# Reading a weight matrix in short contiguous runs in one stage of a fused decode kernel

## The chip, the cores and the metric

The kernel runs on one core of one Trainium2 chip. The metric is device time in microseconds (us) of one execution. A "fast run" is an execution whose time lies close to the fastest of the same kernel; only fast runs are compared.

## The reference, cut to what matters

```python
x = A_x; xn = layernorm(x)
return x + A(xn, k_cache, v_cache, wq, wo) + B(xn, w1, w2, w3, w4)

# A: one decode step of attention; batch 4, 32 query heads on 16 KV heads, window 2048, head size 128
#    softmax(q k^T / sqrt(128)) v, then @ wo          (k and v: 33.5 MB each in the window)
# B: x1 = x + shift(gelu(layernorm(x) @ w1)) @ w2
h2 = gelu(layernorm(x1) @ w3) @ w4                    # w3: 576 x 4608, w4: 4608 x 576
return x1 + h2
```

All data are bf16. With four rows of activations almost every byte that is loaded is used once: 88.5 MB come from HBM.

## The kernel before

One queue of loads (issued by SyncE) fills a ring of four positions with K chunks 1 to 16, then V chunks 1 to 16, 2 MB each. TensorE (PE) transposes each K chunk, ScalarE and VectorE copy it out of PSUM, and PE computes the scores. A ring position is loaded again when its last chunk has been transposed:

```python
for c in range(NC):     # NC = 16, NPOS = 4
    add_dma(kv_pairs(A_k_cache, c), ("k", c % NPOS), [t_done(c - NPOS)] if c >= NPOS else [], c)
for c in range(NC):
    add_dma(kv_pairs(A_v_cache, c), ("v", c % NPOS), [f"PV{c - NPOS}" if c >= NPOS else t_done(c + NC - NPOS)], KS + c)
```

So the fifth K chunk can be asked for only when PE has finished with the first. The MLP stage B stands on PE ahead of the K loop. Its second layer (h2) multiplies by w3, which lies in SBUF as rows of 4608 columns. w4 is loaded later in five pieces, whose partitions hold 18, 9, 6, 2 and 1 consecutive rows of w4. To match that order the kernel gathers columns of w3: for one row of w4 per partition it reads every 18th (9th, 6th, ...) column.

```python
W4_ROWS = (18, 9, 6, 2, 1)
H2ps = [ps[:, 4 + k, 0:384] for k in range(3)]
...
def pe_h2(r):                                   # r: one of 5 blocks of up to 128 rows of w3
    def f(e):
        for g, k, off, cnt, base_, rc, rr, first in sorted(segs, key=lambda x: (x[1], x[2], x[0])):
            w, x_ = ...                         # [cut]
            ins = e.matmul(H2ps[k][32 * g:32 * g + 32, 128 * off:128 * (off + cnt)].rearrange("p (c x) -> p c x", c=cnt), lhsT=x_,
                           rhs=w.rearrange("p (x s) -> p s x", s=rc)[:, rr:rr + cnt, :], start=(r == 0 and first), stop=(r == 3),
                           tile_position=(0, 32 * g), skip_group_check=True)
        return ins
    return f
for n, r in enumerate((0, 1, 4, 2, 3)):         # blocks 2 and 3 need the second half of w3
    add("pe", pe_h2(r), waits=[ev_w3[r // 2]] + ...)
# then: three GELUs (ScalarE), nine 128x128 transposes (PE), and the K loop
```

`tile_position=(0, 32 * g)` runs the four matmuls of a group side by side, so four streams are read at once: in the trace the first four start within 0.01 us of one another, and the records overlap (65 matmuls of 0.76 us each on average fill 11.1 us).

## Time and profile before

215.10 us median of six runs (214.99 to 215.34). The table is read from the page and the timeline of the kernel before.

| what | value |
|---|---|
| bytes loaded, mean rate over the span | 88.65 MB, 415 GB/s |
| PE, VectorE, ScalarE busy | 68%, 35%, 28% of the span |
| h2 matmuls (65) | 4.48 + 6.63 = 11.1 us |
| nine transposes of h2 | 0.68 us |
| K loop starts; fifth K chunk is issued | 38.8 us; 45.2 us |

From the page, the busy times and the 40 slices of the span (a digit is the busy share in tenths):

```profile
PE 144.9 (68%) x2639; PEld 110.3 (52%) x2643; DVE 75.3 (35%) x147; ACT 60.3 (28%) x76; POOL 10.9 (5%) x38
...
PE   0048698899999999999997077233444433336985
...
PEclk9999999699999999999999755555555555555899
DMA  7999999999999999999999999999999999999993
GB/s 282 406 383 449 435 415 436 426 420 425 433 429 420 429 433 433 422 429 429 423 429 433 423 429 423 421 436 426 426 423 436 426 423 426 433 429 429 427 413 129
```

The DMA engines are full in every slice but the first and the last. No engine comes near that over the whole span, but PE is as full in the 13 slices from 43 to 112 us, which lie in the K loop.

The chain of waits that ended last, its end (start us, length us, what):

```profile
178.12 32.27 DMA w<-in_B_w_dram
...
210.43 1.35 PE ps L433 x18
211.78 0.43 DVE out_sb L554
```

The last thing that the kernel waits for is a piece of w4. The timeline where the change acts (start us, length us, engine, line, operation, shapes, count, and in brackets the engine's idle time just before, with what ended it):

```profile
24.68 4.48 PE L517 MATMUL ps<-w,x1nT 128*32 128x384 bf16 x26 [0.38 <-DMA w<-in_B_w_dram]
...
30.06 6.63 PE L517 MATMUL ps<-w,x1nT 128*32 128x384 bf16 x39
...
36.74 1.25 ACT L526 ACTIVATE PT<-ps 128x384 bf16<-128x384 f32 x3 [10.17 <-remote]
...
38.05 0.68 PE L532 MATMUL ps<-ident_bf,PT 128*128 128x128 bf16 x9 [1.36 <-ACT PT L526]
...
38.82 3.45 PE L335 MATMUL ps<-perm_bf,ring 128*128 128x128 bf16 x32
...
45.18 9.90 SPq L175 DMA_DIRECT2D ring<-in_A_k_cache_dram  x3
```

L517 are the h2 matmuls, L526 the GELUs, L532 the transposes of h2, L335 the first transposes of K. The last line is the queue: at 45.18 it issues the fifth K chunk.

### The profile page before, as it was taken

The page shows a single profiled execution, that of the slowest core. Times are in us where ns is not written, and L with a number is a line of the kernel's source. Part 1 is how long each engine was busy: PE and PEld are TensorE (multiplying, and loading weights), DVE is VectorE, ACT ScalarE, POOL GpSimd, SP SyncE. Part 2 cuts the span into 40 slices and gives each one's busy share as a digit, 9 for nine tenths or more (in the row PEclk, how much of TensorE's full clock was granted, in tenths as well). Part 3 has the DMA queues.
Part 4 walks back from the last instruction along what each step waited for, and adds up shares of the span by engine and source line. Part 5 has one row for each costly group of instructions (what it writes and reads, how often), then busy time and mean ns, then how long its engine had stood idle before and what let it go on. Part 6 is the DMA issues. An engine that isn't in the chain of part 4 may idle for free. (4 is left out here: it accounts for less than half of the span.)

```text
span 213.6 us, 5856 instructions
## 1 busy us (share of the span) xinstructions
PE 144.9 (68%) x2639; PEld 110.3 (52%) x2643; DVE 75.3 (35%) x147; ACT 60.3 (28%) x76; POOL 10.9 (5%) x38
## 2 busy tenths in 40 slices
PE   0048698899999999999997077233444433336985
PEld 0023332778888877888885047233434433334542
DVE  0243600366677677667764741100010001001000
ACT  2001401355666665566666540000000000000000
POOL 8301000001000000100000000000000000000000
PEclk9999999699999999999999755555555555555899
DMA  7999999999999999999999999999999999999993
GB/s 282 406 383 449 435 415 436 426 420 425 433 429 420 429 433 433 422 429 429 423 429 433 423 429 423 421 436 426 426 423 436 426 423 426 433 429 429 427 413 129
DMA packets 6690, 88.65 MB, mean 415 GB/s; under 512 B 780, under 2 KB 1048, under 8 KB 1560
## 3 DMA queue, kind: packets, MB, share of 16 engines
q1 hardware_dynamic: 6664, 88.50, 97.8%
q8 instruction: 8, 0.13, 0.2%
q14 instruction: 2, 0.02, 0.0%
q10 hardware_dynamic: 16, 0.01, 0.0%
HBM read 88.49 MB, written 0.00 MB: 414 GB/s over the span
## 5 line engine op out<-in xcount | busy, mean ns | idle before, releaser
L335 PEld LDWEIGHTS ps<-perm_bf,ring 128*128 128x128 bf16 x1024 | 59.0, 99 | 7.2 <-issue 7.0
L335 PE MATMUL ps<-perm_bf,ring 128*128 128x128 bf16 x1024 | 62.0, 222 | 0.1
L342 DVE COPY kt<-ps 128x1024 bf16<-128x1024 bf16 x80 | 52.4, 688 | 24.5 <-PE ps L335 23.3
L416 PE MATMUL ps<-PTpad,ring 128*128 128x8 bf16 x1024 | 29.7, 168 | 40.6 <-PEq L578 36.8
L341 ACT ACTIVATE kt<-ps 128x1024 bf16<-128x1024 bf16 x48 | 47.6, 1023 | 29.9 <-PE ps L335 29.9
L416 PEld LDWEIGHTS ps<-PTpad,ring 128*128 128x128 bf16 x1024 | 28.7, 104 | 41.7 <-issue 41.6
L555 ACT ACTIVATE out_sb<-ps 4x288 bf16<-4x288 f32 x1 | 0.4, 401 | 86.6 <-PE ps L433 86.6
L349 PE MATMUL ps<-kt,Qs 128*32 128x512 bf16 x272 | 17.8, 382 | 1.4 <-PEq L578 1.4
L405 DVE TENSOR_TENSOR PTpad<-PT,mU_bf 128x512 bf16<-128x512 bf16 x16 | 6.4, 422 | 29.0 <-PE ps L416 29.0
L428 DVE TENSOR_TENSOR OTn<-ps,rinvB 128x32 bf16<-128x32 f32 x4 | 0.8, 192 | 34.2 <-PE ps L416 34.2
L517 PE MATMUL ps<-w,x1nT 128*32 128x384 bf16 (+1 forms) x65 | 11.1, 760 | 0.4 <-DMA w<-in_B_w_dram 0.4
L276 PE MATMUL ps<-ident_bf,xn_bf 4*128 4x4 bf16 x8 | 0.6, 170 | 13.8 <-DVE ragsrc L270 13.8
L349 PEld LDWEIGHTS ps<-kt,Qs 128*32 128x32 bf16 x272 | 5.8, 95 | 6.8 <-issue 1.5
L370 POOL COPY Qs<-Qpad 128x128 bf16<-128x128 bf16 x16 | 4.6, 296 | 88.2 <-PE ps L349 74.7
L276 PEld LDWEIGHTS ps<-ident_bf,xn_bf 4*128 4x128 bf16 x8 | 0.4, 112 | 13.9 <-issue 11.5
L517 PEld LDWEIGHTS ps<-w,x1nT 128*32 128x32 bf16 x65 | 3.6, 109 | 5.4 <-issue 4.7
L433 PE MATMUL ps<-w,h2T_sb 128*4 128x288 bf16 x72 | 4.9, 286 | 1.3 <-DMA w<-in_B_w_dram 1.3
L554 DVE CAST out_sb<-ps 4x288 bf16<-4x288 f32 x1 | 0.4, 446 | 14.5 <-PE ps L433 14.5
L433 PE MATMUL ps<-w,ORT 128*4 128x288 bf16 x64 | 4.9, 321 | 0.4 <-DVE ORT L455 0.4
L387 PE MATMUL ps<-kt,permT_bf 128*128 128x512 bf16 x3 | 1.8, 609 | 4.9 <-DVE kt L386 4.8
L433 PEld LDWEIGHTS ps<-w,h2T_sb 128*4 128x4 bf16 x72 | 2.9, 84 | 3.7 <-DMA w<-in_B_w_dram 2.7
L538 DVE COPY h2T_sb<-ps 128x16 bf16<-128x16 bf16 x1 | 0.2, 166 | 13.0 <-PE ps L532 13.0
(99 smaller groups left out, 63.5 us busy)
## 6 DMA issues: line engine op xcount, KB each, us to landing
ring<-in_A_k_cache_dram SPq DMA_DIRECT2D x16, 2048.0 KB, 12.3
ring<-in_A_v_cache_dram SPq DMA_DIRECT2D x16, 2048.0 KB, 17.1
w<-in_B_w_dram SPq DMA_DIRECT2D x2, 2304.0 KB, 22.6
w<-in_A_wo_dram SPq DMA_DIRECT2D x2, 2304.0 KB, 20.6
kt<-in_A_wq_dram SPq DMA_DIRECT2D x1, 4096.0 KB, 12.5
w<-in_B_w_dram SPq DMA_DIRECT2D x1, 2592.0 KB, 28.0
w<-in_B_w_dram SPq DMA_DIRECT2D x3, 576.0 KB, 13.9
w<-in_B_w_dram SPq DMA_DIRECT2D x1, 1296.0 KB, 30.6
```

Source lines behind the costliest of these rows:

```text
L276: e.transpose(XTps[idx][:, r, :], v[:, r, :], ident_bf[0:B, 0:B])
L335: ins = e.transpose(tb[n % 4][:, t, :], slot_t(c)[:, 8 * k + t, :], perm_bf[:])
L341: return "act", lambda e: e.activation(out=ktbuf[:, n % 16], in_=tb[n % 4], func=ACTF.Copy)
L342: return "dve", lambda e: e.tensor_copy(out=ktbuf[:, n % 16], in_=tb[n % 4])
L349: ins = e.matmul(Sps[32 * u:32 * u + 32, q, :].rearrange("p (t i) -> p t i", t=16), lhsT=Qs[:, c % NPOS, 32 * u:32 * u + 32], rhs=ktgrp[:, ...
L370: P(lambda e, c=c, cc=cc: e.tensor_copy(out=Qs[:, c % NPOS, :], in_=Qpad_t[:, 128 * cc:128 * cc + 128]), waits=["qT", "qs_zero"] + ([f"SC{ ...
L387: add("pe", lambda e, q=q: e.matmul(ps[:, 4 + q % 3, :], lhsT=permT_bf[:], rhs=PTx[:, q, :], start=True, stop=True), waits=[f"PTx{q}", "pe ...
L405: return lambda e: e.tensor_tensor(out=PTpad[:, c % 2], in0=PTv[:, :, cc, :].unsqueeze(2).to_broadcast([128, NT, NU, 2]), in1=mU_bf[:].uns ...
L416: ins = e.matmul(o_, lhsT=slot_t(c)[:, t, :], rhs=PTpad[:, c % 2, t].rearrange("p u e -> p (u e)"), start=(t == 0), stop=(t == NT - 1))
L428: add("dve", lambda e, hv=hv: e.tensor_tensor(out=hv(OTn), in0=OTps.rearrange("p (b h) -> p b h", b=B), in1=hv(rinvB), op=ALU.mult), waits ...
L433: return e.matmul(ACC[h], lhsT=lhsT, rhs=rhs, start=start, stop=stop, tile_position=(0, 32 * h), skip_group_check=True)
L517: ins = e.matmul(H2ps[k][32 * g:32 * g + 32, 128 * off:128 * (off + cnt)].rearrange("p (c x) -> p c x", c=cnt), lhsT=x_, rhs=w.rearrange(" ...
```

## The change

It exchanges the order of the two inner loops of the read. A matmul takes a third of the positions x (43, 43 or 42) and for each of them up to nine neighbouring columns, so w3 is read in runs of 9 (or 6, 2, 1). PSUM and the GELU's output are then ordered by position first, and each transpose takes every ninth column. There are 90 h2 matmuls instead of 65. No load changes.

```diff
+        XS = (0, 43, 86, 128)
+        H2ps = [ps[:, 4 + k, 0:9 * (XS[k + 1] - XS[k])] for k in range(3)]
...      # segs: runs of up to 9 columns of one row group of w4, no longer cut in threes
+                for k in range(3):
+                    for g, off, cnt, base_, rc, rr in sorted(segs, key=lambda x: (x[1], x[0])):
-                    ins = e.matmul(H2ps[k][32 * g:32 * g + 32, 128 * off:128 * (off + cnt)].rearrange("p (c x) -> p c x", c=cnt), lhsT=x_,
-                                   rhs=w.rearrange("p (x s) -> p s x", s=rc)[:, rr:rr + cnt, :], start=(r == 0 and first), stop=(r == 3),
+                        ins = e.matmul(H2ps[k][32 * g:32 * g + 32, :].rearrange("p (x c) -> p x c", c=9)[:, :, off:off + cnt], lhsT=x_,
+                                       rhs=w[:, base_:base_ + 128 * rc].rearrange("p (x s) -> p x s", s=rc)[:, XS[k]:XS[k + 1], rr:rr + cnt],
+                                       start=(r == 0 and off == 0), stop=(r == 3), ...
-            ... out=h2g[:, 384 * k:384 * (k + 1)], in_=H2ps[k], func=ACTF.Gelu_apprx_tanh
+            ... out=h2g[:, 9 * XS[k]:9 * XS[k + 1]], in_=H2ps[k], func=ACTF.Gelu_apprx_tanh
-                ins = e.transpose(..., h2g[:, 128 * j:128 * j + 128], ident_bf[:])
+                ins = e.transpose(..., h2g[:, j:1152:9], ident_bf[:])
```

More of the change, by code (lines that the diff above doesn't have):

```diff
@@ L140, in bass_parallel_sum__sliding_block_cached__mixer_s_mlp__decode_kernel @@
         QTps = ps[:, 6, :].bitcast(BF16)
-        H2ps = [ps[:, 4 + k, 0:384] for k in range(3)]
+        XS = (0, 43, 86, 128)
+        H2ps = [ps[:, 4 + k, 0:9 * (XS[k + 1] - XS[k])] for k in range(3)]
         H2Ta = ps[:, 7, :].bitcast(BF16)
@@ L499, in bass_parallel_sum__sliding_block_cached__mixer_s_mlp__decode_kernel @@
         for g in range(4):
-            for k in range(3):
-                first = 9 * g + 3 * k
-                t = first
-                while t < first + 3:
-                    n = next(m for m, (a, z) in enumerate(W4N) if a <= t < z)
-                    cnt = min(first + 3, W4N[n][1]) - t
-                    segs.append((g, k, t - first, cnt, w4cols[W4N[n][0]][0], W4_ROWS[n], t - W4N[n][0], t == first))
-                    t += cnt
+            t = 9 * g
+            while t < 9 * g + 9:
+                n = next(m for m, (a, z) in enumerate(W4N) if a <= t < z)
+                cnt = min(9 * g + 9, W4N[n][1]) - t
+                segs.append((g, t - 9 * g, cnt, w4cols[W4N[n][0]][0], W4_ROWS[n], t - W4N[n][0]))
+                t += cnt
         def pe_h2(r):
@@ L511, in f @@
                 ins = None
-                for g, k, off, cnt, base_, rc, rr, first in sorted(segs, key=lambda x: (x[1], x[2], x[0])):
-                    if r < 4:
-                        w, x_ = w3r[r][:, base_:base_ + 128 * rc], x1nT[:, r, :]
-                    else:
-                        w, x_ = ragq3[:, base_:base_ + 128 * rc], x1nT[:, 4, :]
-                    ins = e.matmul(H2ps[k][32 * g:32 * g + 32, 128 * off:128 * (off + cnt)].rearrange("p (c x) -> p c x", c=cnt), lhsT=x_,
-                                   rhs=w.rearrange("p (x s) -> p s x", s=rc)[:, rr:rr + cnt, :], start=(r == 0 and first), stop=(r == 3),
-                                   tile_position=(0, 32 * g), skip_group_check=True)
+                for k in range(3):
+                    for g, off, cnt, base_, rc, rr in sorted(segs, key=lambda x: (x[1], x[0])):
+                        w, x_ = (w3r[r], x1nT[:, r, :]) if r < 4 else (ragq3, x1nT[:, 4, :])
+                        ins = e.matmul(H2ps[k][32 * g:32 * g + 32, :].rearrange("p (x c) -> p x c", c=9)[:, :, off:off + cnt], lhsT=x_,
+                                       rhs=w[:, base_:base_ + 128 * rc].rearrange("p (x s) -> p x s", s=rc)[:, XS[k]:XS[k + 1], rr:rr + cnt],
+                                       start=(r == 0 and off == 0), stop=(r == 3), tile_position=(0, 32 * g), skip_group_check=True)
                 return ins
@@ L525, in bass_parallel_sum__sliding_block_cached__mixer_s_mlp__decode_kernel @@
         for k in range(3):
-            add("act", lambda e, k=k: e.activation(out=h2g[:, 384 * k:384 * (k + 1)], in_=H2ps[k], func=ACTF.Gelu_apprx_tanh), waits=["h2_3"],
+            add("act", lambda e, k=k: e.activation(out=h2g[:, 9 * XS[k]:9 * XS[k + 1]], in_=H2ps[k], func=ACTF.Gelu_apprx_tanh), waits=["h2_3"],
                 sig="gelu2" if k == 2 else None, key=-0.9 + 0.1 * k)
@@ L531, in pe_h2T @@
             for j in range(9):
-                ins = e.transpose(H2Ta[:, 128 * j:128 * j + 128] if j < 8 else H2Tb, h2g[:, 128 * j:128 * j + 128], ident_bf[:])
+                ins = e.transpose(H2Ta[:, 128 * j:128 * j + 128] if j < 8 else H2Tb, h2g[:, j:1152:9], ident_bf[:])
             return ins
```

## The prediction

> **What bounds the kernel.** Its loads. The page's slices show the DMA engines at 90% or more from the second slice to the last but one; 2 us windows from 20 to 208 us show a DMA share of 0.92 to 1.07 and 387 to 456 GB/s; the page gives 88.65 MB at a mean of 415 GB/s, which is the 213.6 us span. The chain of waits agrees: 15% of the span, the last 32 us, is the final w4 load (landing at 210.4), then 1.8 us of matmuls and copy. [...] PE is busy 68%, DVE 35%, ACT 28%.
>
> **Where the change acts.** Only in the MLP block between 24.7 us (w3's first half has landed) and 38.8 us (first K transpose). By the timeline: 65 h2 matmuls, 4.48 + 6.63 = 11.1 us; three GELUs 1.25 us; nine transposes 0.68 us. Four 384-column matmuls take 0.53 to 0.70 us there, while four 512-column matmuls of the scores, reading runs of 32 elements, take about 0.21 us. The strided read of w3 (every 18th, 9th or 6th column) costs. [...]
>
> **Costs.** The change makes 90 matmuls of 65 (some of only 86 or 43 columns, scattered in PSUM), but most read runs of 9 or 6 columns. Estimate from these numbers: 0.3 us per group of six, 15 groups: 4 to 6 us, not 11.1. The transposes load every ninth column as weights: estimate 0.7 to 2 us, not 0.68. No DMA changes.
>
> **How much of it is critical.** First, the last two row blocks wait for w3's second half, which lands at 31.0 us, so the h2 matmuls end at about 33 us, not 36.7. GELUs to 34.4, transposes to about 35.5. The first K chunk lands only at 36.0, so the K loop starts near 36 instead of 38.8: 2.5 to 3 us of PE time won. Second, that wins no load time. K chunks land every 4.9 us; PE needs 4.68 us each and before ran behind them (last chunk landed 109.8, its transposes ended 115.4). After, PE waits for the loads; scores end about 115.5, not 117.8. Refills only queue earlier on a queue that is never empty: the fifth K chunk is issued at 45.2, the fourth lands at 50.9.
>
> **Predicted time.** 215.1 us, range 214.4 to 215.8. Faster by over 2%: 1.5%; within 2%: 97%; slower by over 2%: 1.5%.
>
> **What would show it right.** The h2 matmul group falls from 11.1 us to under 7 us; PE waits for a load between the row blocks until 31 us; K transposes start at 35.5 to 37 us and the K loop shows waits for K chunks; landing times of K, V and w4 stay within 0.5 us; the chain's tail is again w4.
>
> **What would make it wrong.** If small PSUM-scattering matmuls or strided weight loads cost far more than estimated, so that h2 ends over 4 us later than before, the fifth K chunk is issued too late, the queue runs dry once and the bubble reaches the end. If the queue had gaps that 2 us windows hide, earlier issues could win up to a microsecond.

Two sentences are cut from the prediction, at the marks: a rate of the DMA side and a rule for the reads, which no trace or run of this case shows. 215.10 us before, less nothing, because the 2.5 to 3 us of PE time win no load time, came to 215.1 us. The "4 to 6 us" is 15 groups at 0.3 us, 4.5 us, the author's estimate from the 0.53 to 0.70 and 0.21 us quoted there.

## More of the kernel before

A single look (one execution with a profile) has the state "unknown" and is read for its trace, not for a small difference in time.

The DMA view of 20 to 208 us gives the rate that this study uses:

```profile
DMA packets 5519, 80.32 MB, mean 427 GB/s; under 512 B 611, under 2 KB 611, under 8 KB 694
```

## The result, and the profile after

215.09 us median of six runs (214.93 to 215.19) against 215.10 us. The ratio is 0.9998, with a 95% interval of 0.9985 to 1.0011: the same. (A ratio here is the mean time of one kernel's fast runs over that of the other's fast runs of the same rounds, so it is not quite the ratio of the quoted medians.)

The page of the kernel after:

```profile
PE 141.4 (66%) x2664; PEld 110.4 (52%) x2668; DVE 75.3 (35%) x147; ACT 61.2 (29%) x76; POOL 10.8 (5%) x38
...
PE   0038683999999999999996277133444433336995
...
PEclk9999999799999999999999655555555555555799
DMA  7999999999999999999999999999999999999993
GB/s 282 406 385 449 438 411 442 414 429 422 432 426 429 429 423 435 422 432 420 439 423 432 420 425 427 427 426 435 426 423 426 429 429 426 429 429 436 426 404 124
```

Its DMA view of 20 to 208 us, and the end of its chain of waits:

```profile
DMA packets 5516, 80.30 MB, mean 427 GB/s; under 512 B 611, under 2 KB 611, under 8 KB 692
```

```profile
178.16 32.29 DMA w<-in_B_w_dram
...
210.49 1.36 PE ps L434 x18
211.86 0.43 DVE out_sb L551
```

The loads run at the same rate and the same piece of w4 ends the kernel, 0.06 us later. The timeline where the change acts (L514 h2 matmuls, L523 GELUs, L529 transposes of h2, L336 transposes of K):

```profile
26.61 1.51 PE L514 MATMUL ps<-w,x1nT 128*32 128x387 bf16 x36 [0.35 <-DVE x1nT L494]
...
29.56 2.17 PE L514 MATMUL ps<-w,x1nT 128*32 128x387 bf16 x54
...
31.76 1.26 ACT L523 ACTIVATE PT<-ps 128x387 bf16<-128x387 f32 x3 [3.23 <-PE ps L514]
...
33.07 0.76 PE L529 MATMUL ps<-ident_bf,PT 128*128 128x128 bf16 x9 [1.35 <-ACT PT L523]
...
36.27 2.89 PE L336 MATMUL ps<-perm_bf,ring 128*128 128x128 bf16 x32 [2.44 <-PEq L575]
...
42.71 5.22 SPq L176 DMA_DIRECT2D ring<-in_A_k_cache_dram  x2
```

The h2 matmuls take 1.51 + 2.17 = 3.7 us in place of 11.1, a third. The transposes of h2 end at 33.83 us instead of 38.73, 4.9 us earlier. Then PE stands idle for 2.44 us: the first K chunk lands at 35.98 us (from the trace's landing records; 35.95 before). The page names PE's sequencer as the releaser, because in the loop the wait for a chunk is an instruction of the sequencer's own (L575, `wait_ge`).

The starts of PE's work on the K chunks, from the traces, show how the rest of the lead goes:

```
chunk          1     2     3     4     5  ...   9    10    11  ...   15     16   last ends
before us   38.8  45.0  49.7  54.4  59.1      77.8  82.5  87.2      105.9  110.6   115.40
after us    36.3  42.5  47.2  52.0  56.7      75.5  80.4  85.3      104.8  109.7   114.55
```

PE alone needs 4.68 us for a chunk; the loads bring one every 4.9 us. Before, PE ran behind the loads through the whole loop. After, it has caught up with them at the ninth chunk, and from there it follows their pace. The lead of 2.5 us shrinks to 0.85 us. The V chunks land at the same times, to 0.3 us, in both traces; from the third V chunk on (124.42 and 124.41 us) the difference is under 0.1 us.

One difference in these two traces does not belong to the change. The h2 matmuls start 1.9 us later after (26.6 against 24.7 us) because the matmuls of w2 ahead of them ran at half clock: one group of four took 1.12 us instead of 0.65 (240 ns from start to start, not 122), and the trace's clock records have the full clock from 23.4 us, not from 18.1. The clock does not change at the same moments in the two traces later either: the next half-clock stretch of the kernel before starts at 38.6 us and that of the kernel after at 37.05, and each lasts 3.41 us. Why was not shown. (The PEclk rows of the pages show a 9 before 18.1 and 23.4 us because the clock records only start there.) In the traces of eleven of the twelve experiments below, with either kernel's code, the h2 matmuls start between 24.4 and 25.6 us; in the twelfth they start at 26.4.

### The profile page after: what moved, and what is told of

Read it like the earlier page. It is cut to its first block, busy times and chain, and to the rows that moved or that the text cites. A ratio compares the mean times of both kernels' runs of the same rounds, so it can differ in the third digit from the quotient of the medians.

```text
span 213.7 us, 5906 instructions
## 1 busy us (share of the span) xinstructions
PE 141.4 (66%) x2664; PEld 110.4 (52%) x2668; DVE 75.3 (35%) x147; ACT 61.2 (29%) x76; POOL 10.8 (5%) x38
## 5 line engine op out<-in xcount | busy, mean ns | idle before, releaser
L336 PE MATMUL ps<-perm_bf,ring 128*128 128x128 bf16 x1024 | 62.5, 221 | 3.0 <-PEq L575 2.4
L336 PEld LDWEIGHTS ps<-perm_bf,ring 128*128 128x128 bf16 x1024 | 58.3, 98 | 11.3 <-issue 11.1
L342 ACT ACTIVATE kt<-ps 128x1024 bf16<-128x1024 bf16 x48 | 48.4, 1023 | 33.0 <-PE ps L336 32.3
L350 PE MATMUL ps<-kt,Qs 128*32 128x512 bf16 x272 | 18.5, 393 | 1.4 <-PEq L575 1.4
L434 PE MATMUL ps<-w,ORT 128*4 128x288 bf16 x64 | 5.8, 358 | 0.4 <-DVE ORT L456 0.4
L264 ACT ACTIVATE sd<-mv 4x1 f32<-4x1 f32 x3 | 0.6, 202 | 15.8 <-DVE mv L262 15.8
L434 PEld LDWEIGHTS ps<-w,ORT 128*4 128x4 bf16 x64 | 3.4, 106 | 3.0 <-DVE ORT L456 1.0
L440 PE MATMUL ps<-zeros_bf 128*128 128x512 bf16 x13 | 3.8, 419 | 0.4 <-DVE OTn L429 0.2
```

Source lines behind the costliest of these rows:

```text
L336: ins = e.transpose(tb[n % 4][:, t, :], slot_t(c)[:, 8 * k + t, :], perm_bf[:])
L342: return "act", lambda e: e.activation(out=ktbuf[:, n % 16], in_=tb[n % 4], func=ACTF.Copy)
L350: ins = e.matmul(Sps[32 * u:32 * u + 32, q, :].rearrange("p (t i) -> p t i", t=16), lhsT=Qs[:, c % NPOS, 32 * u:32 * u + 32], rhs=ktgrp[:, ...
L434: return e.matmul(ACC[h], lhsT=lhsT, rhs=rhs, start=start, stop=stop, tile_position=(0, 32 * h), skip_group_check=True)
L440: ins = e.matmul(ps[:, 3, :], lhsT=zeros_bf[:, 0:128], rhs=zeros_bf[:, :], start=True, stop=True)
```

## The experiments

Two theories stood at the start. **Theory L**: the loads bound the kernel; the change shortens PE work that has slack in front of the loads, so what it wins is slack, not time. **Rival G**: PE time counts, and the gain was given back by slower PE work later. The page after does show the score matmuls at a mean of 393 ns against 382, and those of wo at 358 against 321, so G needed a test. (The clock records do explain both means. Only the scores of the first K chunk differ, 580 against 382 ns, and most of their time lies in the half-clock stretch from 37.05 to 40.46 us. The late half-clock stretch lasts until 200.9 us after and 199.0 before, and the wo matmuls run from 197.3 to 203.2 and 202.2.) A third question was why the reads got faster: by the order of the reads from SBUF (theory A), or by the order of the writes to PSUM or the number of matmuls (theory B).

### What made the h2 matmuls fast: reads, writes, or length of the run

Three kernels, one look each. `strided_read` is the kernel after with the old order of reads; it then writes PSUM with a step of 9:

```diff
-  ... .rearrange("p (x c) -> p x c", c=9)[:, :, off:off + cnt], lhsT=x_,
-  rhs=w[...].rearrange("p (x s) -> p x s", s=rc)[:, XS[k]:XS[k + 1], rr:rr + cnt],
+  ... .rearrange("p (x c) -> p c x", c=9)[:, off:off + cnt, :], lhsT=x_,
+  rhs=w[...].rearrange("p (x s) -> p s x", s=rc)[:, rr:rr + cnt, XS[k]:XS[k + 1]],
```

> The kernel after, but w3 is read column by column again (every 18th, 9th or 6th), and each column is written with a step of 9 in PSUM. Theory A (the order of the reads from SBUF sets the time of the h2 matmuls): about 11 us for the h2 matmuls, as before, with 90 matmuls instead of 65. Theory B (the order of the writes to PSUM, or the number of matmuls, sets it): clearly more than 11 us, or clearly less if the number of columns per matmul was the point. Total about 215.1 us under either.

`psum_scatter` reads the runs but writes each element 43 columns from the last; the GELUs put the order right, and the transposes are contiguous again:

```diff
-  ... .rearrange("p (x c) -> p x c", c=9)[:, :, off:off + cnt], lhsT=x_,
+  ... .rearrange("p (c x) -> p x c", c=9)[:, :, off:off + cnt], lhsT=x_,
-  out=h2g[:, 9 * XS[k]:9 * XS[k + 1]], in_=H2ps[k]
+  out=h2g.rearrange("p (c x) -> p c x", c=9)[:, :, XS[k]:XS[k + 1]], in_=H2ps[k].rearrange("p (c x) -> p c x", c=9)
-  h2g[:, j:1152:9]
+  h2g[:, 128 * j:128 * j + 128]
```

> The kernel after, with its runs of 9 read from SBUF, but written to PSUM 43 columns apart (transposes contiguous again). Theory A (reads set the time): the h2 matmuls stay near 3.7 us. Theory B (writes set it): they go well over 5 us, towards 11. The nine transposes: 0.68 us as before, if their 0.76 us after came from the step of 9. Total about 215.1 us.

`runs3` cuts the runs to three columns:

```diff
-  cnt = min(9 * g + 9, W4N[n][1]) - t
+  cnt = min(9 * g + 9, W4N[n][1], t + 3) - t
```

> The kernel after with runs of at most 3 columns: 195 matmuls of 129 or fewer columns in place of 90. [...] If any run longer than one column is enough: about 4 us. If the cost is one for each matmul: about 8 us. Total about 215.1 us.

Measured: all correct; 215.64, 215.10 and 216.14 us, beside 214.92 us for one run of the kernel before. These are single runs, and runs of the kernel before reached 216.5 us and more on some chips, so no difference in total is read from them. The lines of their timelines:

```profile
26.44 4.47 PE L514 MATMUL ps<-w,x1nT 128*32 128x387 bf16 x36 [0.35 <-DVE x1nT L494]
...
31.82 6.65 PE L514 MATMUL ps<-w,x1nT 128*32 128x387 bf16 x54
```

```profile
24.79 2.12 PE L514 MATMUL ps<-w,x1nT 128*32 128x387 bf16 x36 [0.35 <-DVE x1nT L494]
```

```profile
31.14 1.98 PE L514 MATMUL ps<-w,x1nT 128*32 128x129 bf16 x78 [1.63 <-DMA w<-in_B_w_dram]
```

The first fence is `strided_read`, the second `psum_scatter`, the third `runs3`; of the last two one part that ran at full clock is shown, two of the five blocks of rows. For two blocks the kernel before takes 4.48 us and the kernel after 1.51, both at full clock. The first line of `strided_read` did not run at full clock: the records have half clock from 26.41 to 29.83 us, most of its time. It still took 4.47 us, and so did the same blocks in `before_idle40` (4.49 us, half clock from 25.54 to 28.96), while fast reads slow down with the clock (2.74 us at half clock in `after_idle60`, 1.51 at full). So the clock of TensorE did not set the pace of the single-column reads here.

| two blocks of rows | reads | writes to PSUM | us |
|---|---|---|---|
| before | single columns | contiguous | 4.48 |
| strided_read | single columns | step of 9 | 4.47 |
| psum_scatter | runs of 9 | step of 43 | 2.12 |
| runs3 | runs of 3 | runs of 3, step of 9 between them | 1.98 |
| after | runs of 9 | contiguous, mostly | 1.51 |

Theory A holds in the main: with single-column reads the time stays at the old value (4.47 against 4.48 us, and 6.65 against 6.63 for the other three blocks, at full clock), though there are 25 more matmuls and the writes are scattered. But the writes are not free: once the reads are fast, a step of 43 in PSUM costs 40% (2.12 against 1.51 us), which theory A alone did not expect. All h2 matmuls of `psum_scatter` together took 6.8 us, part of it at half clock (the granted clock was 0.91 on average from 20 to 40 us), or 5.3 at full clock (an estimate, 2.12 times 2.5): over the 3.7 that theory A had named and, at full clock, barely over the 5 that theory B had set as its least. Runs of three already bring most of the gain: 1.98 us for two blocks, or about 5 us for the five (an estimate, 1.98 times 2.5; 5.9 us of busy time in this run, where the first two blocks took 2.87 us and the granted clock was 0.85 on average from 20 to 40 us). That is 1 us above the expectation if any run were enough, and far from the 8 us of a cost per matmul (an estimate, 3.7 us times 195/90). A third expectation, 5 to 6.5 us, is cut from the record: it rested on a rule for the reads that no run here shows. What the writes of `runs3` add is not separated. The nine transposes took 0.68 us in `psum_scatter`, so the step of 9 costs them 0.08 us.

### Load taken away

`after_no_wo1` leaves out the second half of wo; `after_halfv` loads V chunks 9 to 12 by half. Their outputs are wrong, which doesn't matter for the times.

```diff
-  ... ["h2_3"], KS + WO_AT[h]) for h in range(2)]
+  ... ["h2_3"], KS + WO_AT[h]) for h in range(1)] * 2
```

> The kernel after without the load of the second half of wo (wrong result on purpose). Theory (the loads bound the kernel): 2.36 MB less at 0.427 MB/us, so 5.5 us less, about 209.6 us. Rival (a chain of PE, ACT and DVE work bounds it, and the h2 gain was given back there): within 1 us of 215.

```diff
-  add_dma(kv_pairs(A_v_cache, c), ("v", c % NPOS), ...
+  pr = kv_pairs(A_v_cache, c)
+  if 8 <= c < 12:
+      pr = [(o_[:, 0:UE // 2], i_[:, :, 0:UE // 2]) for o_, i_ in pr]
+  add_dma(pr, ("v", c % NPOS), ...
```

> The kernel after with V chunks 9 to 12 loaded by half (4.2 MB less; wrong result on purpose). The run without half of wo took load away after the last V chunk, where the PE work of the tail stands only 1.6 us behind. Here the load is taken away ahead of it. Theory (loads bound the kernel up to the last V chunk): 4.2 MB at 0.427 MB/us is 9.8 us less, about 205.3 us. Rival (PE, ACT and DVE work sets the time): within 2 us of 215.

Measured: `after_no_wo1` 213.36 us in one look, 1.56 us less than the run of the kernel before beside it; the theory had expected 5.5 us less. Its chain of waits has no load in it:

```profile
193.65 1.86 PE ps L417 x64
...
197.29 5.51 PE ps L434 x68
...
202.96 1.46 PE ps L440 x6
204.42 2.30 PE ps L434 x36
206.72 1.19 PE ps L440 x5
207.90 2.35 PE ps L434 x36
210.25 0.43 DVE out_sb L551
```

The last pieces of w4 land at 205.9 us there, 5.6 us earlier than in the kernel after, as the rate of the loads had promised. But PE is not ready for them: after the last V chunk it still has the products with V, wo and w4 to do (L440 are matmuls on zeros, part of the kernel's design). So behind the last loads stands a second chain, only about 1.6 us shorter. This run therefore settles little between L and G, and it corrects L: the loads bound the kernel up to the last V chunk, and from there two chains of nearly the same length run to the end.

`after_halfv` takes load away ahead of that point: 205.35 us median of four runs (205.28 to 205.48), ratio to the kernel before 0.954, interval 0.951 to 0.957. The theory had said 205.3. Its chain ends with w4 again:

```profile
168.52 32.27 DMA w<-in_B_w_dram
...
200.83 1.36 PE ps L437 x18
202.19 0.43 DVE out_sb L554
```

With the same PE, VectorE and ScalarE work, 4.2 MB less load is 9.7 us less time. That is theory L.

### PE time added ahead of the K loop

If the change buys slack, a burden of PE time should show it. Matmuls on zeros were put between the transposes of h2 and the K loop, in both kernels:

```diff
   add("pe", pe_h2T, waits=["gelu2"], sig="h2T", key=-0.6)
+  add("pe", pe_idle(40), waits=["zeros_bf"], sig=None, key=-0.4)      # 24, 40 or 60
```

> The kernel before, with 40 dense matmuls on zeros (512 columns, about 0.216 us each, 8.6 us) between the h2 transposes and the K loop. Theory (loads bound it; PE time ahead of the K loop is free until the fifth K chunk is issued too late): the K loop starts near 47.4 us, the fifth K chunk is issued near 53.8, the queue has run dry at 50.7, so with about 1 us from issue to first packet the total rises by about 4 us, to 219. Rival (PE time counts in full, and the change's gain was given back by slower PE work later): plus 8.6 us, 223.7.

> The kernel after with the same 40 matmuls at the same place. Theory: the K loop starts near 42.5 us, the fifth K chunk is issued near 48.9, before the queue runs dry at 50.7: total 215.1 to 215.8 us, so about 4 us less than the kernel before under the same burden. Rival (PE time counts in full): near 223.7.

> The kernel after with 60 such matmuls (12.9 us). Theory: the K loop starts near 46.8 us, the fifth K chunk is issued near 53.2, a gap of about 3.5 us in the loads: total about 218.6 us. Rival (PE time counts in full): about 228.

> The kernel before with 24 idle matmuls (5.2 us at 0.216 us each) ahead of the K loop. Refined theory, from the runs with 40 and 60: a burden is free until the fifth K chunk is issued later than about 47.9 us (the loads' share falls at about 48.8, and the first packets follow an issue by 0.9), and a late issue costs its lateness and about 1 us for filling the queue again. Without a burden that issue stands at 45.2, so 2.7 us are free: about 2.5 us left over, plus 1: 217.6 to 218.6 us. Rival (PE time counts in full): 220.3. Rival (PE time is free): 215.1.

> The kernel after with the same 24 idle matmuls. Refined theory: the h2 transposes end near 35.5 us, the K loop starts near 40.7 instead of 36.3, the fifth K chunk is issued near 47, just inside 47.9: 215.1 to 215.8 us, at least 2 us less than the kernel before under the same burden. Rival (PE time counts in full from the end of the transposes): 219 to 220.

Measured (median, and ratio to the kernel before of the same rounds with its interval; the times of K loop and issue are those of the profiled run; "added" is the median less that of the kernel before of the same rounds, 215.10 or 215.01 us):

| kernel | us | ratio | added us | K loop starts | fifth K chunk issued |
|---|---|---|---|---|---|
| before_idle24 | 219.37 | 1.020 (1.017 to 1.023) | 4.4 | 43.6 | 48.4 |
| after_idle24 | 216.01 | 1.005 (1.001 to 1.010) | 1.0 | 40.2 | 45.0 |
| before_idle40 | 223.73 | 1.038 (1.034 to 1.042) | 8.6 | 49.7 | 54.6 |
| after_idle40 | 218.65 | 1.015 (1.011 to 1.019) | 3.6 | 45.8 | 50.6 |
| after_idle60 | 222.88 | 1.037 (1.032 to 1.042) | 7.8 | 48.0 | 52.8 |

Under the same burden the kernel after is faster by 3.4 us with 24 matmuls and by 5.1 us with 40. The gain of the change is there; without the burden nothing asks for it.

The sizes were off: `before_idle40`, `after_idle40` and `after_idle60` came 4.7, about 3 and 4.3 us above what the theory had said. `before_idle40` landed on 223.7 us, the number that the rival had named, though not for its reason. If PE time counted in full, `after_idle40` would have been near 223.7 too; it was 5 us below. And the trace of `before_idle40` shows the loads standing still. Windows of `before_idle40` and then of `after_idle40` (length, busy times, granted clock, DMA share, GB/s):

```profile
46.00:48.00 2.00, 2.00 (x11) 0.88 (x9) 0.00 (x0) 0.00 (x0) 0.00 (x0) 1.00 0.98 418
48.00:50.00 2.00, 2.00 (x14) 1.05 (x13) 0.00 (x0) 0.00 (x0) 0.00 (x0) 1.00 0.37 147
50.00:52.00 2.00, 2.00 (x39) 1.74 (x40) 1.41 (x3) 1.02 (x1) 0.00 (x0) 1.00 0.00 0
52.00:54.00 2.00, 2.00 (x41) 1.51 (x30) 0.86 (x2) 0.75 (x1) 0.29 (x1) 1.00 0.00 0
54.00:56.00 2.00, 2.00 (x39) 1.99 (x37) 1.72 (x4) 1.68 (x3) 0.00 (x0) 1.00 0.31 74
56.00:58.00 2.00, 2.00 (x36) 1.26 (x34) 1.25 (x2) 0.60 (x2) 0.29 (x1) 1.00 0.82 319
```

```profile
46.00:48.00 2.00, 2.00 (x39) 1.75 (x40) 1.40 (x3) 1.02 (x1) 0.00 (x0) 1.00 0.96 410
48.00:50.00 2.00, 2.00 (x41) 1.50 (x30) 0.86 (x2) 0.73 (x1) 0.29 (x1) 1.00 0.42 164
50.00:52.00 2.00, 2.00 (x40) 1.99 (x38) 1.72 (x4) 1.68 (x3) 0.00 (x0) 1.00 0.23 66
52.00:54.00 2.00, 2.00 (x36) 1.25 (x34) 1.26 (x2) 0.60 (x2) 0.29 (x1) 1.00 0.84 336
```

Two things were missing in the expectation. First, the burden was longer than counted: from the end of the transposes to the K loop passed 9.9 and 10.3 us, not 8.6, as part of it ran at half clock (in `before_idle40` the granted clock was 0.85 from 42 to 44 us). Second, the queue runs dry earlier than the fourth chunk's landing at 50.9 us: most engines are done at 48.5 us, while the last data packet of that chunk starts at 49.83 and ends at 50.45. And the first packet after the late issue at 54.59 starts at 55.92, 1.3 us later, of which the issue itself lasted 0.54; in `after_idle60` it is 1.3 us too (52.84 to 54.16). The expectation's 1 us is what the kernel before shows for its first load (0.81 to 1.84 us). (The 0.9 us in the expectation for 24 matmuls is what the shares of 2 us windows give: 0.23 of the window from 50 to 52 us puts the start near 51.5, 0.9 us after the issue at 50.60. The packets themselves start at 51.94, again 1.3 us after it.) With these the size can be followed: the fifth chunk lands at 63.8 us instead of 55.9, 7.9 us late, which is most of what was lost. (The profiled run was the slowest of the four, at 225.28 us.) With 48.5 and 1.3 the last issue that costs nothing is at about 47.2 us, an estimate, and not at 47.9. That leaves the kernel before about 2.0 us of slack (its issue is at 45.2) and the kernel after about 4.5 (42.7): the change bought some 2.5 us of it.

The runs with 24 matmuls were chosen on that ground, and came near, not exactly. (Their "about 1 us for filling the queue again" was the author's estimate: `after_idle40` lost 3.6 us with its issue at 50.6, 2.7 us after 47.9. That the rest is filling was not shown.) `before_idle24` lost 4.4 us instead of 2.5 to 3.5; in its trace the share of the loads is 0.72 and 0.80 in the windows from 48 to 52 us, but it is 0.75 once more at 66 to 68, so the queue, once it had run low, lost a little again: the fifth chunk lands 1.5 us later than in the kernel before, the seventh 2.7. `after_idle24` had three runs at 215.06 to 215.20 us, free as expected, and three at 216.8 to 217.7. Those three have the lower granted clock (0.794 to 0.795 against 0.800 to 0.808); a burden that runs longer at half clock would pass the limit, but none of the three was profiled, so that is argued and not shown.

### The loads thinned in the K stage

Here the change should pay in a kernel without a burden. K chunks 5 to 16 are loaded by half, in both kernels. Their outputs are wrong, which doesn't matter for the times.

```diff
+  if c >= NPOS:
+      pr = [(o_[:, 0:UE // 2], i_[:, :, 0:UE // 2]) for o_, i_ in pr]
```

> The kernel before with K chunks 5 to 16 loaded by half (12.6 MB less; wrong result on purpose), all other work as before. Theory (in the K stage PE now sets the pace, and loads do again from the fifth V chunk on): the K loop starts at 38.8 and runs at 4.68 us a chunk as before; the fifth V chunk is issued near 128.3 with the queue just dry, lands near 134.2 in place of 139.7, total about 209.6 us. If loads alone counted: 29 us less, 186.

> The kernel after with the same halved K loads. Theory: the K loop starts at 36.2 (first K chunk's landing), 2.6 us ahead, and nothing makes it wait later, so 2.5 us less than the halved kernel before: about 207.1 us. Here the change should pay. Rival (the gain is given back by slower PE work later): the same time as the halved kernel before, within 0.5 us.

Measured: 214.77 us (214.45 to 215.27) and 211.36 us (210.75 to 212.99), each of four runs. The ratios to the kernel before are 0.996 (0.990 to 1.002), the same, and 0.983 (0.976 to 0.990), which a limit of 2% leaves unclear. But every run of one is below every run of the other. The change pays 3.4 us by the medians, against 2.5 expected; in the profiled runs the K loop starts 2.7 us earlier and the fifth V chunk lands 3.0 us earlier (135.54 against 138.56). Rival G had said within 0.5 us, and falls.

The absolute times were wrong: 12.6 MB less saved `before_halfk` next to nothing. The windows show why, for `before_halfk`:

```profile
70.00:80.00 10.00, 10.00 (x176) 8.38 (x176) 6.97 (x12) 6.56 (x7) 0.59 (x2) 1.00 0.64 223
```

The loads idle through a third of the K stage, but the stage lasts as long as before, because PE needs 4.68 us a chunk against the loads' 4.9. The first four V chunks are issued at 101.6 to 115.7 us (101.4 to 115.4 without the cut) and the loads are busy from there, so the fifth V chunk lands at 138.6 us, only 1.1 us earlier. The expectation had let the first V chunks land at once. The lesson is that load and PE are nearly balanced in the K stage, and each hides a gain in the other.

## Why the prediction was right

- **Total.** 215.1 us was predicted and 215.09 measured. `after_halfv` and the burden pairs show that it was right for its reason: the loads bound the kernel, and the change bought PE slack.
- **h2 matmuls.** "4 to 6 us, not 11.1": measured 3.7 us in the profile after, a little under the range, and, from one experiment to another with the same h2 code, up to 5.1 us where part of it ran at half clock. The reason, that single columns are slow to read and runs are not, was shown by `strided_read`: two blocks took 4.47 us there, where neighbouring reads lie up to 18 columns apart, 1.98 in `runs3` and 1.51 in the kernel after.
- **Transposes.** "0.7 to 2 us", the upper end an estimate without a run behind it: measured 0.76. The strided weight load itself rose from 98 to 144 ns, but transposes start every 60 ns instead of 56, so almost all of it overlaps.
- **PE waits for w3's second half until 31 us.** Not in the profile after, where the half landed at 29.9 us and the stage started late at half clock. It is there in experiments with the same h2 code: in `after_halfv` PE idles 2.55 us until 31.19, and in `after_idle24` 2.87 us until 31.54.
- **K loop.** It starts at 36.3 us (35.5 to 37 was predicted), held by the landing of the first K chunk. That PE would wait for the loads through the whole loop was too strong: it catches up with them only at the ninth chunk.
- **Scores.** "About 115.5": measured 116.95, against 117.8 before. The step that was mis-sized is the time from the last landing to the end: PE's 4.8 us for a chunk contain the scores of the chunk before it, and the prediction counted the transposes alone.
- **Landings within 0.5 us.** True of K, V and w4 (0.3 us at most).
- **The margin.** The prediction warned of an h2 that ends "over 4 us later". The margin was smaller: `before_idle24` starts the K loop 4.8 us late and pays over 4 us. The landing of the fourth chunk was taken for the time when the queue runs dry; most engines are done some 2 us before it.
- **Not seen.** The PE chain behind the last V chunk, 1.6 us short of the loads, was not in the prediction. It did not matter for this change, but it would cap any saving of load at the end.

## What to carry to other kernels

Before a faster PE stage is counted as time, ask what it lets start earlier, and whether that resource is idle then: here it let loads be queued earlier on a queue that was never empty. A change that wins only slack can still be worth keeping; measure the slack by adding a burden to both kernels, and the time by thinning the loads. For the reads themselves: put even a short contiguous run innermost, as three columns won most of what nine did here (1.98 and 1.51 us for two blocks, 4.48 with single columns), and keep the writes to PSUM contiguous as well (a step of 43 took 2.12 us against 1.51).
